# Float16 high and low parts, slots by products and array quarters in a fused attention and mixture-of-experts kernel

## The chip, the cores and the metric

The kernel runs on one core of a Trainium2 chip. The metric is device microseconds for one execution. PE is TensorE, DVE VectorE, ACT ScalarE, POOL GpSimd, SP the engine that issues plain transfers.

## The reference

Local and global attention over q, k, v of shape (4, 8, 768, 64): a query sees the 96 keys that end at itself and the first 8 keys, with a bias that falls with distance. The result, 3072 tokens of 512 numbers, goes through a mixture of eight experts, of which each token takes two:

```python
scores = scale * np.matmul(q, k.transpose(0, 1, 3, 2)) + bias
scores = np.where(keep, scores, -1e9)              # keep = global | local
a = np.exp(scores - max); a = a / (sum + 1e-9)
x = np.matmul(a, v)                                # as (3072, 512)
noisy = x @ w_gate + np.log1p(np.exp(x @ w_noise)) * noise
top2, top2_w = the two largest of 8, softmax of them
for e in range(8):                                 # w1 (8,512,1024), w2 (8,1024,512)
    h = np.maximum(x[mask] @ w1[e], 0.0)
    out[mask] += top2_w * (h @ w2[e])
```

## The kernel before

**Attention.** The work is cut into 24 groups of 128 tokens; a group has four pairs of heads, 96 pairs in all. For a pair, `score` multiplies two blocks of 64 queries with a window of 168 keys (line 480; the first group of each of the 4 batches has 128 keys), in fp32. The two heads of a pair share one product: the query tile `qbuf` holds one head in its upper, the other in its lower 64 rows, with zeros beside them. An fp32 product appears in the trace as two passes on PE. Vector adds the bias and finds the maximum (line 483), Scalar takes the exponential (line 487). `trans` turns the probabilities with four PE transposes per pair (line 499), Scalar copies them out (line 501), `attend` multiplies them with v and a column of ones (line 519, four fp32 products of 65 columns), and Vector divides (lines 525 to 528). The order of each engine is written out by hand in one loop over pairs: transposes of pair n, scores of pair n+2, then `attend` of pair n-2.

**Gate and routing.** After a group's last pair `gate_t`, `gate_l` and `gate_s` turn its tokens, multiply them with the gate weights and leave logits. `gate_l` (line 193) already uses tile positions: four products, each in its own 32 columns of the array. The generator `route`, run a step at a time between other work (`tick`), picks two experts per token for a run of groups (`SEG`), gives each entry a slot, and POOL scatters token number and weight into a table in DRAM (line 297), which is read back.

**Experts.** For each expert e, 812 slots: 512 as part c=0, 300 as part c=1, gathered from DRAM by POOL in seven tiles (`gather`) and turned by PE in fp32 (`turn`, line 164). Precision is kept with float32r pairs: x, w1, h and w2 are split into a high part (Scalar) and the rest (Vector, `split`), and every product is three: high by high, high by low, low by high. `up` (line 693) makes h, `down` and `down_t` (lines 726 and 736) the output, `back` (line 746) turns part c=1 back, and `put` adds rows into the output in DRAM by an indirect transfer (line 711). Per expert: 96 products of 512 and 96 of 300 columns in `up`, as many in `down` and `down_t`. Weights come as 1 MB halves into three `raw` buffers, issued by SP. While expert e is multiplied, its w2, the next w1 and the next tokens are split.

Of the kernel before, what the change touches and what calls it, by code (L numbers as in the profile page):

```python
# [10 lines left out]
F32 = mybir.dt.float32  # L11
# [11 lines left out]
TA = 4  # L23
TB, MB = 3, 100
CA, CB = TA * P, TB * MB
CAP = CA + CB
DUMP = 512


@with_exitstack  # L30
def tile_local_global_attention_then_moe(
# [25 lines left out]
    TS = N + P  # L57
# [4 lines left out]
    SEG = [(0, 6), (6, 12), (12, 17), (17, 21), (21, NT)]  # L62
# [14 lines left out]

    xd = dram.tile([N + DUMP, Dm], F32, name="xd")
    tbl = dram.tile([E * TS, 2], I32, name="tbl")
    slots = tbl.rearrange("(e r) c -> e r c", e=E)  # L80

    zero = consts.tile([P, Dm], F32, name="zero")
    ident = consts.tile([P, P], F32, name="ident")
    noise_s = consts.tile([P, NT, E], F32, name="noise_s")
# [7 lines left out]
    tok = consts.tile([P, NT, 2], I32, name="tok")  # L92
    tb0 = consts.tile([P, TA, 2], I32, name="tb0")
    tba = consts.tile([P, E, TA, 2], I32, name="tba")
    tbb = consts.tile([MB, E, TB, 2], I32, name="tbb")
    more = consts.tile([1, E + 1], I32, name="more")

    w1h = wts.tile([P, KC, F], FR, name="w1h")
    w1l = wts.tile([P, KC, F], FR, name="w1l")
    xh = [wts.tile([P, KC, CA], FR, name="xh0")]  # L100
    xl = [wts.tile([P, KC, CA], FR, name="xl0")]
# [6 lines left out]
    def load_w(n=1):  # L108
        for _ in range(n):
            if len(asked) == len(order):  # L110
                return
            x, e, h = order[len(asked)]
            asked.append(order[len(asked)])
            if x == 1:
                t = wts.tile([P, KC, F // 2], F32, name="raw", tag="raw", bufs=3)
                src = w1[e, :, h * F // 2:(h + 1) * F // 2].rearrange("(k p) f -> p k f", p=P)
            else:
                t = wts.tile([P, FC // 2, Dm], F32, name="raw", tag="raw", bufs=3)
                src = w2[e, h * F // 2:(h + 1) * F // 2].rearrange("(k p) d -> p k d", p=P)
            nc.sync.dma_start(t, src)  # L120
            raw[x, e, h] = t

    def split(e, x, j, eng=nc.vector):

        t = raw[x, e, j // 4]
        if x == 1:
            t = t[:, :, (j % 4) * P:(j % 4 + 1) * P]
            hi, lo = (y[:, :, j * P:(j + 1) * P] for y in (w1h, w1l))
        else:
            t, hi, lo = t[:, j % 4], w2h[:, j], w2l[:, j]  # L130
        nc.scalar.activation(hi, t, AF.Copy)  # L131
        eng.tensor_sub(lo, t, hi.bitcast(F32))  # L132
        if j % 4 == 3 and (e or x == 2):
            load_w()

    xg = {}

    def rows(e, t):

        if t >= TA:  # L140
            return tbb[:, e, t - TA]
        return tba[:, e, t] if e else tb0[:, t]

    def gather(e, t, n=DUMP + N):
        r = rows(e, t)
        xg[e, t] = gp.tile([r.shape[0], Dm], F32, name="xg", bufs=5)
        nc.gpsimd.indirect_dma_start(
            out=xg[e, t], out_offset=None, in_=xd[:n],
            in_offset=bass.IndirectOffsetOnAxis(ap=r[:, 0:1], axis=0),
# [4 lines left out]
    def spare_bank():  # L154
        spare[0] += 1
        return bank("m" if spare[0] % 2 else "lg", 1)

    def turn(e, t, ps=None):
        x = xg.pop((e, t))
        m = x.shape[0]  # L160
        c, c0 = (0, t * P) if t < TA else (1, (t - TA) * MB)
        ps = (spare_bank() if ps is None else ps)[:, :KC * m].rearrange("p (k t) -> p k t", k=KC)
        for k in range(KC):
            nc.tensor.transpose(ps[:, k], x[:, k * P:(k + 1) * P], ident[:m, :m])
        cols = slice(c0, c0 + m)
        nc.scalar.activation(xh[c][:, :, cols], ps, AF.Copy)
        nc.vector.tensor_sub(xl[c][:, :, cols], ps, xh[c][:, :, cols].bitcast(F32))  # L167

    NZ = 8
# [10 lines left out]
    def gate_t(g):  # L180
        x = XR.pop(g).rearrange("p h d -> p (h d)")
        nc.sync.dma_start(xd[DUMP + g * P:DUMP + (g + 1) * P], x)
        ps = bank("m", 1).rearrange("p (k t) -> p k t", k=KC)
# [5 lines left out]
    def gate_l(g):  # L189
        ps = bank("m", 1)[:, :P]  # L190
# [13 lines left out]
    def route(r):  # L204
# [56 lines left out]
        ent = small.tile([P, SW, 2, 2], I32, name=f"ent{r % 2}")[:, :w]  # L261
        we = ent[:, :, :, 1].bitcast(F32)
        nc.vector.reciprocal(we[:, :, 0], wt[:, :, 0])
        nc.vector.tensor_copy(ent[:, :, :, 0], tok[:, a:z])
        yield
        nc.vector.tensor_mul(we[:, :, 1], wt[:, :, 1], we[:, :, 0])
        yield
        ps = lg[:, NT * 2 * E:]
# [13 lines left out]
        nc.vector.tensor_add(po, po, slot0[:, :w])  # L282
# [8 lines left out]
        sli = small.tile([P, SW, 2], I32, name=f"sli{r % 2}")[:, :w]  # L291
        nc.vector.tensor_copy(sli, sl)
        for i in range(w):
            for _ in range(2 if r else 4):
                yield
            for j in range(2):
                ins = nc.gpsimd.indirect_dma_start(
                    out=tbl, out_offset=bass.IndirectOffsetOnAxis(ap=sli[:, i, j:j + 1], axis=0),
                    in_=ent[:, i, j], in_offset=None, bounds_check=E * TS - 1, oob_is_err=False)
                for o in scat:  # L300
                    tc.declare_no_dep(ins.ins, o.ins, reason="each entry has a slot of its own")
                scat.append(ins)
        if r == CLOSE:

            nc.vector.tensor_scalar(carry[:, 0:1], carry[:, 0:1], float(CA), None, op0=OP.max)
            nc.gpsimd.dma_start(tb0, slots[0, :CA].rearrange("(p t) c -> p t c", t=TA))
            for _ in range(12):
                yield
            for t in range(TA):
                gather(0, t, DUMP + z * P)  # L310
                yield

    scat = []


    with ExitStack() as actx:
# [8 lines left out]
        def load_qk(b, j, i0):  # L325

            if i0 == 0:
                qs[b, j] = qbuf[j]
# [23 lines left out]
        if windowed:  # L352
            vpb = [ac.tile([NP + NG, HD], F32, name=f"vp{j}") for j in range(4)]
            qbuf = [ac.tile([P, 2 * NBH, KC, 2, Q], F32, name=f"qbuf{j}") for j in range(2)]
            load_qk(0, 0, 0)
# [32 lines left out]
            def clear(e, j, n):  # L388
                for x in range(2):
                    e.memset(qbuf[j][(1 - x) * D:(2 - x) * D, n, :, x], 0.0)  # L390

# [3 lines left out]
            clear(nc.vector, 0, slice(0, 2))  # L395
# [16 lines left out]
            AW = WIN + Q  # L412
            abuf = [ac.tile([P, 2, AW], F32, name=f"a{j}") for j in range(4)]
            for t in abuf:
                for x in range(2):
                    nc.gpsimd.memset(t[:, x, (1 - x) * WIN:(1 - x) * WIN + Q], 0.0)
            clear(nc.gpsimd, 0, slice(2, 2 * NBH))
# [3 lines left out]
        if windowed:  # L421
            load_v(2)
            clear(nc.gpsimd, 1, slice(0, 2 * NBH))

        def gate_consts():
            nc.vector.memset(wgn, 0.0)
# [5 lines left out]
        def route_consts():  # L432
# [8 lines left out]
            nc.gpsimd.iota(slot0, pattern=[[0, SW], [TS, E]], base=0, channel_multiplier=0,  # L441
                           allow_small_or_imprecise_dtypes=True)
            nc.gpsimd.iota(tok, pattern=[[P, NT], [0, 2]], base=DUMP, channel_multiplier=1)

        def empty_table():
            nc.gpsimd.memset(zero, 0.0)
            j = E * TS // P
            ent0 = ac.tile([P, j, 2], I32, name="ent0")
            nc.gpsimd.memset(ent0, 0)
            nc.gpsimd.iota(ent0[:, :, 0], pattern=[[1, j]], base=0, channel_multiplier=j)  # L450
            nc.vector.tensor_scalar(ent0[:, :, 0], ent0[:, :, 0], DUMP - 1, None, op0=OP.bitwise_and)
            nc.sync.dma_start(tbl.rearrange("(p j) c -> p j c", p=P), ent0)
            o = xd[:DUMP].rearrange("(p r) d -> p r d", p=P)
            nc.sync.dma_start(o, zero[:, None, :].to_broadcast(o.shape))
# [6 lines left out]
        def tick():  # L461
            beat[0] += 1
            active[:] = [(x, r) for x, r in active if r < CLOSE and beat[0] % 2 or next(x, 0) is None]
# [6 lines left out]
        def score(n):  # L470
            g, hp, b, i = geo(n)
            w = WIN if i else P
            j, i0 = divmod(i, NBH)
            ps = bank("sc", 2)[:, :2 * w].rearrange("p (s w) -> p s w", s=2)
            ns = aw.tile([P, 2, WIN], F32, name="ns", bufs=3)
            mx = aw.tile([P, 2], F32, name="mx", bufs=4)
            A[n] = abuf[n % 4]
            for s in range(2):
                k0 = i0 * KB + s * Q if i else NP + NG
                nc.tensor.matmul(ps[:, s], qs[b, j][:, 2 * i0 + s, hp], ks[b, j][:, hp, k0:k0 + w],  # L480
                                 start=True, stop=True)
            for s in range(2):
                nc.vector.tensor_tensor_reduce(  # L483
                    out=ns[:, s, :w], in0=ps[:, s], in1=bias[:, hp, s] if i else bias0[:, hp, s],
                    scale=-scale, scalar=3e38, op0=OP.add, op1=OP.min, accum_out=mx[:, s:s + 1])
                c = s * Q if i else AW - P
                nc.scalar.activation(A[n][:, s, c:c + w], ns[:, s, :w], AF.Exp, bias=mx[:, s:s + 1], scale=-1.0)  # L487
                tick()

        def trans(n):  # L490
            g, hp, b, i = geo(n)
            w = 2 * P if i else P
            ps = bank("at", 2)[:, :2 * w]
# [404 lines left out]
```

## Time and profile before

| | us |
|---|---|
| median of 3 runs (lowest, highest) | 862.3 (860.43, 867.2) |
| profiled execution, first to last instruction | 824.2 |
| attention stage, to the first product of expert 0 | 0 to 207 |
| experts, to the last product | 207 to 813 |
| period of one expert in the middle (439.60 to 514.51) | 74.9 |

The runs' time covers more than the span that the profile shows: the median lies 38.1 us above it. The page gives the busy time of each engine; the timeline gives starts, and the distance from one product's start to the next is its real price, since products overlap and their ends are modelled.

### The profile page before, as it was taken

How to read it: one execution, taken by the hardware profiler on the slowest of the kernel's cores; microseconds unless marked ns; L12 is line 12 of the kernel's file. 1: busy time of each engine (PE TensorE's matmuls, PEld its weight loads, DVE VectorE, ACT ScalarE, POOL GpSimd, SP SyncE). 2: the span in 40 equal slices, each digit the busy share in tenths (PEclk: the TensorE clock that was granted, in tenths of full speed). 3: DMA queues.
4: the chain of work that ended last, by engine and by line, in shares of the span. 5: the costliest groups of instructions: out<-in, count | busy, mean ns of one | idle time of the engine just before them, and what ended most of it. 6: DMA issues, size and time to landing. Idle time of an engine off the chain costs nothing. (4 is left out here: it accounts for less than half of the span.)

```text
span 824.2 us, 14072 instructions
## 1 busy us (share of the span) xinstructions
PE 800.4 (97%) x5265; PEld 722.0 (88%) x5265; DVE 323.9 (39%) x1116; ACT 346.9 (42%) x736; POOL 228.4 (28%) x219
## 2 busy tenths in 40 slices
PE   6999999999998999999999999999999999999994
PEld 6999999999787989898888989898988889898983
DVE  6446656656731434133323423342333334233400
ACT  5778777676422443233333323333333333223311
POOL 4002250353637140314122221403141231302023
PEclk9999999999999999999999999999999999999997
DMA  9899698795366252434343443524443543432014
GB/s 218 215 284 292 163 194 191 176 211 156 116 130 125 66 148 72 108 115 94 113 101 84 120 96 78 139 87 79 121 116 95 100 90 106 96 78 30 2 24 62
DMA packets 86663, 100.73 MB, mean 122 GB/s; under 512 B 35626, under 2 KB 48170, under 8 KB 86586
## 3 DMA queue, kind: packets, MB, share of 16 engines
q1 hardware_dynamic: 71322, 73.05, 33.0%
q0 software_dynamic: 15264, 26.69, 18.0%
q8 instruction: 44, 0.72, 0.4%
q14 instruction: 33, 0.27, 0.1%
HBM read 71.46 MB, written 28.24 MB: 121 GB/s over the span
## 5 line engine op out<-in xcount | busy, mean ns | idle before, releaser
L711 POOL DMA_INDIRECT out_dram<-y,tba x28 | 44.6, 1592 | 257.2 <-ACT y L710 257.2
L726 PE MATMUL av<-w2h,hh 128*128 128x512 f32 x256 | 102.7, 401 | 0.0
L726 PE MATMUL av<-w2h,hl 128*128 128x512 f32 x256 | 101.3, 396 | 0.0
L726 PE MATMUL av<-w2l,hh 128*128 128x512 f32 x256 | 101.1, 395 | 0.0
L132 DVE TENSOR_TENSOR w1l<-raw,w1h 128x512 fp32r<-128x512 f32 x56 | 38.3, 690 | 148.0 <-ACT w1h L131 148.0
L487 ACT ACTIVATE a<-ns,mx 128x168 f32<-128x168 f32 (+1 forms) x192 | 73.0, 423 | 39.8 <-DVE mx L483 38.0
L693 PE MATMUL sc<-xh,w1h 128*128 128x512 f32 (+1 forms) x256 | 89.6, 350 | 0.0
L693 PE MATMUL at<-xh,w1h 128*128 128x512 f32 (+1 forms) x256 | 89.4, 349 | 0.0
L693 PE MATMUL at<-xl,w1h 128*128 128x512 f32 (+1 forms) x256 | 88.6, 346 | 0.3 <-DVE xl L167 0.3
L693 PE MATMUL at<-xh,w1l 128*128 128x512 f32 (+1 forms) x256 | 88.7, 346 | 0.0
L693 PE MATMUL sc<-xh,w1l 128*128 128x512 f32 (+1 forms) x256 | 88.6, 346 | 0.0
L693 PE MATMUL sc<-xl,w1h 128*128 128x512 f32 (+1 forms) x256 | 88.5, 346 | 0.0
L483 DVE CUSTOM_DVE_ANT_0 ns<-sc,bias 128x168 f32<-128x168 f32 (+1 forms) x192 | 55.7, 322 | 71.2 <-ACT at L501 33.8
L711 POOL DMA_INDIRECT out_dram<-y,tbb x24 | 38.2, 1591 | 147.2 <-ACT y L710 146.8
L736 PE MATMUL av<-hh,w2h 128*128 128x300 f32 x256 | 78.9, 308 | 0.0
L736 PE MATMUL av<-hl,w2h 128*128 128x300 f32 x256 | 76.9, 300 | 0.0
L736 PE MATMUL av<-hh,w2l 128*128 128x300 f32 x256 | 76.9, 300 | 0.0
L704 DVE SCALAR_TENSOR_TENSOR hl<-sc,hh 128x300 fp32r<-128x300 f32 (+1 forms) x62 | 35.8, 578 | 102.9 <-ACT hh L703 102.9
L480 PE MATMUL sc<-ks,qbuf 128*128 128x168 f32 (+1 forms) x384 | 70.0, 306 | 5.8 <-DMA qbuf<-in_q 5.8
L703 ACT ACTIVATE hh<-sc 128x300 fp32r<-128x300 f32 (+1 forms) x62 | 31.5, 508 | 100.1 <-PE sc L693 100.1
L710 ACT ACTIVATE y<-av,tba 128x512 f32<-128x512 f32 x28 | 19.3, 689 | 125.4 <-issue 106.2
L519 PE MATMUL av<-vs,at 128*128 128x65 f32 x384 | 70.7, 273 | 0.0
(144 smaller groups left out, 1679.6 us busy)
## 6 DMA issues: line engine op xcount, KB each, us to landing
raw<-in_w SPq DMA_DIRECT2D x32, 1024.0 KB
out_dram<-zero SPq DMA_DIRECT2D x14, 512.0 KB
vs<-in_v SPq DMA_DIRECT2D x24, 260.0 KB
qbuf<-in_q SPq DMA_DIRECT2D x48, 128.0 KB
xd<-xr SPq DMA_DIRECT2D x24, 256.0 KB
ks<-in_k SPq DMA_DIRECT2D x20, 272.0 KB
vp<-in_v SPq DMA_DIRECT2D x20, 195.0 KB
ks<-in_k SPq DMA_DIRECT2D x4, 464.0 KB
```

What stands on the lines that cost most here:

```text
L132: eng.tensor_sub(lo, t, hi.bitcast(F32))
L480: nc.tensor.matmul(ps[:, s], qs[b, j][:, 2 * i0 + s, hp], ks[b, j][:, hp, k0:k0 + w], start=True, stop=True)
L483: nc.vector.tensor_tensor_reduce(out=ns[:, s, :w], in0=ps[:, s], in1=bias[:, hp, s] if i else bias0[:, hp, s], scale=-scale, scalar=3e38, ...
L487: nc.scalar.activation(A[n][:, s, c:c + w], ns[:, s, :w], AF.Exp, bias=mx[:, s:s + 1], scale=-1.0)
L519: nc.tensor.matmul(ps[:, h % 4], x[:kk, s * w + c0:s * w + c0 + P], t[:kk, c], start=kk < P or not i, stop=kk == P)
L693: nc.tensor.matmul(ps, w[:, k, fs], x[c][:, k], start=n == 0, stop=n == 3 * KC - 1)
L703: nc.scalar.activation(hh[c][:, f], ps, AF.Relu)
L704: nc.vector.scalar_tensor_tensor(hl[c][:, f], ps, 0.0, hh[c][:, f].bitcast(F32), op0=OP.max, op1=OP.subtract)
L710: nc.scalar.activation(y, ps, AF.Copy, scale=r[:, 1:2].bitcast(F32))
L711: ins = nc.gpsimd.indirect_dma_start(out=out, out_offset=bass.IndirectOffsetOnAxis(ap=r[:, 0:1], axis=0), in_=y, in_offset=None, bounds_ch ...
L726: nc.tensor.matmul(ps, x[0][:, f, cols], w[:, f], start=n == 0, stop=n == 3 * FC - 1)
L736: nc.tensor.matmul(ps, w[:, f, cols], x[1][:, f], start=n == 0, stop=n == 3 * FC - 1)
```

## The change

All experts' operands become float16 pairs instead of float32r pairs. So that nothing underflows, each weight matrix gets a scale, a power of two from its largest absolute value (`scales`: Vector reductions over 1024 columns, two small PE operations), and each token row another (`ready`); `put` takes both out again. Gathered tiles are scaled and split on Vector and Scalar before they are turned (`ready`, `rest`), and turned by SP with a transposing transfer from SBUF to SBUF (`turn`); PE turns only expert 0's tiles, in float16 (`turn_pe`). Weights have two sets of buffers and five `raw` buffers. Part c=1 has tiles of 128, 128 and 44 rows.

Slots: no scatter. For each of the 48 entries per lane, Vector and POOL make two one-hot tiles, and PE adds their products into a table in PSUM; `find` reads token numbers off it. A token's weights are stored beside it in `xd`, whose rows grow from 512 to 520 numbers.

Attention goes two pairs at a time. Scores are products of 64 rows and 64 columns in the four quarters of the array, without zeros in q; q is loaded with one transfer where there were two. `trans` turns three squares of 128 per pair where it turned four. `attend` has eight products per pair where it had four, each with 64 output rows, in halves of the array and then in quarters. Scores are made for pairs n+4 and n+5. Four of the eight early `zero_out` transfers move into expert 0.

```diff
-    SEG = [(0, 6), (6, 12), (12, 17), (17, 21), (21, NT)]
+    SEG = [(0, 6), (6, 11), (11, 16), (16, 20), (20, NT)]
...
+    def scales(e, x):
...
+        for i in range(4):
...
+            nc.vector.tensor_reduce(m[:, i:i + 1], t[:, i % 2 * n:(i % 2 + 1) * n], op=OP.max, axis=AX.X,
+                                    apply_absolute_value=True)
+            yield
...
+        nc.tensor.transpose(ps[:4, :P], m, ident)
...
+        nc.tensor.matmul(ps[:, :4], one4, d4, start=True, stop=True)
...
     def split(e, x, j, eng=nc.vector):
...
-        nc.scalar.activation(hi, t, AF.Copy)
-        eng.tensor_sub(lo, t, hi.bitcast(F32))
+        nc.scalar.activation(hi, t, AF.Copy, scale=s)
...
+            eng.scalar_tensor_tensor(lo, t, s, hi, op0=OP.mult, op1=OP.subtract)
...
-            nc.tensor.transpose(ps[:, k], x[:, k * P:(k + 1) * P], ident[:m, :m])
...
-        nc.vector.tensor_sub(xl[c][:, :, cols], ps, xh[c][:, :, cols].bitcast(F32))
...
+    def ready(e, t):
...
+        nc.vector.tensor_reduce(c, x[:, :Dm], op=OP.add, axis=AX.X, apply_absolute_value=True)
+        nc.vector.tensor_scalar(c, c, 2.0 ** (1 - X_UP), TINY, op0=OP.mult, op1=OP.max)
+        nc.vector.tensor_scalar(u.bitcast(I32), c.bitcast(I32), EXP, EXP, op0=OP.bitwise_and, op1=OP.bitwise_xor)
...
+        nc.scalar.activation(y[:m, :Dm], x[:, :Dm], AF.Copy, scale=u)
...
+    def rest(e, t):
...
+        nc.vector.scalar_tensor_tensor(y[:m, Dm:], x[:, :Dm], u, y[:m, :Dm], op0=OP.mult, op1=OP.subtract)
...
+    def turn(e, t):
+        nc.sync.dma_start_transpose(out=place(t, P if t < TT - 1 else MP), in_=xp.pop((e, t)))
...
-                ins = nc.gpsimd.indirect_dma_start(
-                    out=tbl, out_offset=bass.IndirectOffsetOnAxis(ap=sli[:, i, j:j + 1], axis=0),
...
+                (nc.vector if j else nc.gpsimd).tensor_scalar(x, row, slf[:, 0, i, j:j + 1], None, op0=OP.is_equal)
+                nc.vector.tensor_scalar(y, col, slf[:, 1, i, j:j + 1], val[:, a + i:a + i + 1],
+                                        op0=OP.is_equal, op1=OP.mult)
...
+        for i, (x, y) in enumerate(marks):
+            nc.tensor.matmul(ps, x, y, start=i == 0, stop=i + 1 == len(marks))
...
-            for x in range(2):
-                nc.sync.dma_start(qs[b, j][x * D:(x + 1) * D, n, :, x].rearrange("p n k t -> p (n k) t"),
-                                  q[b, j, x, :, n].rearrange("p n k t -> p (n k) t"))
+            nc.sync.dma_start(qs[b, j][:, n], q[b, j].rearrange("x d n k t -> (x d) n k t")[:, n])
...
-                nc.tensor.matmul(ps[:, s], qs[b, j][:, 2 * i0 + s, hp], ks[b, j][:, hp, k0:k0 + w],
-                                 start=True, stop=True)
...
+                for m, ps, i, hp, w, qq, kk, i0 in both:
...
+                    r = slice(hp % 2 * D, (hp % 2 + 1) * D)
+                    for y in range(2):
+                        c = hp // 2 * 2 + y
+                        nc.tensor.matmul(ps[y * Q:(y + 1) * Q, s], qq[r, 2 * i0 + s, c], kk[r, c, k0:k0 + w],
+                                         start=True, stop=True, tile_position=(hp % 2 * D, y * Q))
...
+            cols = (0, 2 * WIN - P, NP + NG) if i else (0, P)
...
-                    nc.tensor.transpose(p4[:, :, c, s * Q:(s + 1) * Q], x[:, s, a:a + P], ident)
...
+                nc.tensor.transpose(ps[:, j * P:(j + 1) * P], x[:, a:a + P], ident)
...
+                    parts = (0, 0, vp[g], 0, NP + NG), (0, 1, vs[g], 0, P), (1, 0, vs[g], 0, Q), (1, 1, vp[g], Q, NP + NG)
...
+            run.sort(key=lambda x: x[:3])
...
+                nc.tensor.matmul(ps[y * Q:(y + 1) * Q, h % 4], w, t, start=id(x) in first, stop=id(x) in final,
+                                 tile_position=(r, y * Q))
...
-            for n in range(NPAIR + LAG):
+            for n in range(0, NPAIR + LAG, 2):
```

## Rows read from the trace of the kernel before

**Rows 1.** The page, part 1: busy us of an engine, share, instructions.

```profile
span 824.2 us, 14072 instructions
...
PE 800.4 (97%) x5265; PEld 722.0 (88%) x5265; DVE 323.9 (39%) x1116; ACT 346.9 (42%) x736; POOL 228.4 (28%) x219
```

**Rows 2.** Busy time by stretch: length, PE, PEld, DVE, ACT, POOL, clock, DMA share, GB/s.

```profile
0.00:205.00 205.00, 197.48 (x1846) 189.65 (x1846) 121.97 (x745) 147.00 (x354) 60.50 (x91) 1.00 0.87 210
205.00:290.00 85.00, 80.20 (x471) 69.86 (x471) 36.36 (x92) 28.32 (x57) 39.30 (x34) 1.00 0.48 113
290.00:740.00 450.00, 450.00 (x2548) 398.52 (x2547) 149.16 (x250) 151.92 (x291) 112.83 (x84) 1.00 0.42 101
```

**Rows 3.** Timeline of PE, one pair in attention: start, us, what.

```profile
129.98 0.64 PE L499 MATMUL at<-ident,a 128*128 128x128 f32 x4
130.46 0.74 PE L480 MATMUL sc<-ks,qbuf 128*128 128x168 f32 x4
131.03 0.33 PE L519 MATMUL av<-vp,at 104*128 104x65 f32 x2
...
131.87 0.60 PE L499 MATMUL at<-ident,a 128*128 128x128 f32 x4
```

**Rows 4.** Timeline of PE around the gate product in column tiles.

```profile
78.24 0.39 PE L519 MATMUL av<-vs,at 128*128 128x65 f32 x2
78.55 0.42 PE L193 MATMUL m<-xt,wgn 128*32 128x128 f32 x8
78.91 0.55 PE L499 MATMUL at<-ident,a 128*128 128x128 f32 x3
```

**Rows 5.** Timeline of PE in `down`, with one turned tile behind it.

```profile
558.18 0.39 PE L726 MATMUL av<-w2h,hl 128*128 128x512 f32 x1
...
562.38 0.40 PE L726 MATMUL av<-w2h,hl 128*128 128x512 f32 x1
562.61 0.60 PE L164 MATMUL lg<-ident,xg 128*128 128x128 f32 x4
562.96 0.48 PE L726 MATMUL av<-w2h,hh 128*128 128x512 f32 x1
563.28 0.39 PE L726 MATMUL av<-w2l,hh 128*128 128x512 f32 x1
```

**Rows 6.** Timeline of PE in `up`, part c=0.

```profile
515.21 0.39 PE L693 MATMUL at<-xh,w1h 128*128 128x512 f32 x1
...
517.02 0.40 PE L693 MATMUL at<-xh,w1l 128*128 128x512 f32 x1
```

**Rows 7.** Timeline of PE in `up`, part c=1.

```profile
539.80 0.30 PE L693 MATMUL sc<-xh,w1h 128*128 128x300 f32 x1
...
541.59 0.30 PE L693 MATMUL at<-xl,w1h 128*128 128x300 f32 x1
```

**Rows 8.** Groups by line and shape, Vector: busy us, mean ns, idle before.

```profile
L704 DVE SCALAR_TENSOR_TENSOR hl<-sc,hh 128x512 fp32r<-128x512 f32 x30 | 20.8, 692 | 64.9 <-ACT hh L703 64.9
L704 DVE SCALAR_TENSOR_TENSOR hl<-sc,hh 128x300 fp32r<-128x300 f32 x32 | 15.1, 471 | 37.9 <-ACT hh L703 37.9
L228 DVE SCALAR_TENSOR_TENSOR p<-p,t 128x40 f32<-128x40 f32 x6 | 1.2, 197 | 0.1
```

**Rows 9.** Transfers by issue: count, median us from issue to landing.

```profile
xg<-xd,tba POOLq DMA_INDIRECT x28, 3.8
out_dram<-y,tba POOLq DMA_INDIRECT x28, 7.6
```

**Rows 10.** The page's transfer rate in 40 slices, and its packets.

```profile
GB/s 218 215 284 292 163 194 191 176 211 156 116 130 125 66 148 72 108 115 94 113 101 84 120 96 78 139 87 79 121 116 95 100 90 106 96 78 30 2 24 62
DMA packets 86663, 100.73 MB, mean 122 GB/s; under 512 B 35626, under 2 KB 48170, under 8 KB 86586
```

More of the change, by code (lines that the diff above doesn't have):

```diff
@@ L768, in tile_local_global_attention_then_moe @@
+            up(0, 0, f, f < 3, {4: gate_t, 8: gate_l, 11: gate_s} if f == 0 and windowed else {})
+            for j in range([0, 0, 0, 2, 3, 4, 6, 7][f], [0, 0, 2, 3, 4, 6, 7, 8][f]):
+                split(0, 2, j)
+        for _ in pending[1]:
+            pass
         for t in range(TB):
             gather(0, TA + t)
-        for t in range(TA - 1):
+        for t in range(2):
+            gather(1, t)
+        weigh(0, 0, TA)
+        for t in range(TA):
             down(0, t)
-        for t in range(TB):
-            turn(0, TA + t, bank("sc", 2) if t == TB - 1 else None)
@@ new lines, in tile_local_global_attention_then_moe @@
+            if t == 1:
+                step(1)
+                for j in range(TB):
+                    ready(0, TA + j)
+                    if j:
+                        rest(0, TA + j - 1)
+                rest(0, TA + 2)
+                for j in range(2, 5):
+                    gather(1, j)
+            if t == 2:
+                step(1)
+                ready(1, 0)
+                step(1, 2)
+            if t == 3:
+                rest(1, 0)
+                turn(1, 0)
+                ready(1, 1)
@@ new lines, in tile_local_global_attention_then_moe @@
+        for t in range(TB):
+            turn_pe(0, TA + t, bank16("sc", 3) if t == TB - 1 else None)
+        for j in range(5, 7):
+            gather(1, j)
+        for f in range(FC):
+            up(0, 1, f)
+            if f in (0, 2, 4):
+                rest(1, 1 + f // 2)
+                turn(1, 1 + f // 2)
+            if f in (0, 2):
+                ready(1, 2 + f // 2)
+            if f == 0:
+                load_w(2)
+            if f not in (0, 2):
+                step(1)
+        ready(1, TA)
@@ new lines, in tile_local_global_attention_then_moe @@
+        for j in range(KC):
+            down_t(0, j)
+            step(1)
+            if j < TB:
+                rest(1, TA + j)
+                turn(1, TA + j)
+                if j + 1 < TB:
+                    ready(1, TA + j + 1)
+        weigh(0, TA, TT)
+        for e in range(1, E):
+            last = e + 1 == E
+            for f in range(FC):
+                up(e, 0, f)
+                if f < TB:
+                    back(e - 1, f)
+                step(e, [0, 0, 0, 1, 0, 1, 2, 2][f])
+                if f == 2 and not last:
+                    for t in range(5):
+                        gather(e + 1, t)
+            weigh(e, 0, TT)
+            for f in range(FC):
+                up(e, 1, f)
+                if f < 2:
+                    step(e, 2)
+                elif f < 6:
+                    step(e + 1)
+                if not last:
+                    if f in (4, 6):
+                        ready(e + 1, f // 2 - 2)
+                    if f in (5, 7):
+                        rest(e + 1, f // 2 - 2)
+                        turn(e + 1, f // 2 - 2)
+                        gather(e + 1, f // 2 + 3)
```

589 lines of the change are left out of this document (343 added, 246 removed).

## The prediction

> **What bounds the kernel now.** I read the page first: PE is busy 97% of the span, Vector 39%, Scalar 42% [rows 1]. Shares over a whole span hide stages, so I looked at stretches next [rows 2]. In attention (0 to 205 us) PE is busy 197 us, but Scalar has 147 and Vector 122 too; in the experts (290 to 740) PE is busy without a break and Vector a third of the time. Third, the timeline of PE, where only starts count. A pair of heads takes 1.89 us from the start of its transposes to the next pair's: 0.48 for four transposes, 0.57 for the scores (four passes of 0.143), 0.84 for eight passes of `attend`, 0.105 each [rows 3]. `attend` streams only 65 columns, and its passes still cost nearly what a transpose of 128 does: loading 128 fp32 columns into the array sets its pace, while the scores go by their stream. In the experts eighteen products of 512 columns in `down` take 4.20 us, 0.233 each [rows 5], eight in `up` 1.81, 0.226 each [rows 6], thirteen of 300 columns 1.79, 0.138 each [rows 7]. The clock is at its full level, 2.4 GHz, in all three stretches [rows 2]. So the kernel is a queue of PE work, and what the change is worth is what it takes out of that queue, until another engine is late.
>
> **Experts.** *Products.* Count and columns stay (512 and 300; three products per float pair), the type changes. At 2.4 GHz 512 columns stream in 0.213 us and 300 in 0.125; the float32r products lie 0.013 to 0.020 above that. No row has a wide float16 product. The bounds: nothing saved (0 us), or all but a small gap. The fp32 scores, which stream too, lie only 0.0025 above their stream (0.1425 against 2 x 168 columns = 0.140) [rows 3], and I take that, as the nearest row that streams without a penalty for the type: 0.216 and 0.1275. Then 768 products in `down` save 0.0173 each (13.3 us), 768 in `up` 0.010 (7.7), 1536 narrow ones 0.010 (15.7): 36.7 us.
>
> *Turning.* A turned tile costs PE from where the next product would have started, 562.61, to 562.96, and the product behind it comes 0.32 later where 0.233 is usual: 0.44 us [rows 5]. 49 tiles (seven experts, seven tiles) leave PE: 21.6 us. They go to SP's queue as transposing transfers. No row shows one. Its landing is bounded by nothing and by some multiple of the two transfers of about the same bytes, 3.8 us for a gathered tile and 7.6 for an added one [rows 9]; I take 4. It is hidden: tile 3 is issued two `down` steps into expert e, six steps before the first product of e+1, some 22 us. On SP each waits for `rest` on Vector, and behind it wait the weight loads, which have five buffers instead of three. Expert 0's seven tiles stay on PE, eight narrow transposes instead of four wide ones: no difference.
>
> *Scales.* Sixteen matrices, each one transpose and one tiny fp32 product, three passes of some 0.11 us as in [rows 3]: 5.3 us added to PE. Their inputs come from Vector one step earlier in program order, with a `down` or an `up` between, so PE doesn't wait.
>
> *Cover.* Vector gains eight reductions over 1024 columns per expert. A row of 512 takes 0.692 us and one of 300 0.471, so a column is 1.04 ns and a reduction 1.22 us: 9.8 us. `ready` adds 7 x (0.69 + two small ones, 0.2 each), 7.6. Vector had 149 us in six experts [rows 2], 25 each; with 2 for the rest 44 of some 68 us. Hidden, if bursts don't hold up the evacuation of PSUM. Sum for the experts: -36.7 - 21.6 + 5.3 = **-53 us**.
>
> **Attention.** I count a double step of two pairs, 3.78 us now. *Transposes*: six instead of eight, 0.72. *Scores*: sixteen quarter passes; if four run side by side, four rounds of 0.143, 0.57. *`attend`*: 32 passes with half the columns to load; two side by side make 16 rounds. A round costs between half of 0.105 (half the columns) and all of it; I take 0.06, near the lower end, since the load sets today's price: 0.96. That parts of the array work side by side is in the trace: `gate_l`'s eight passes in four column tiles take 0.36 us, entry and exit included, where eight passes of `attend` take 0.84 [rows 3, 4]. *Changes of mode* are the price: before those passes PE starts 0.20 after the last product where 0.11 is usual, of the 0.36 some 0.15 is no stream, and the three transposes behind take 0.06 more than theirs [rows 4]: 0.30 for in and out, 0.15 each. A double step has three (halves, quarters, whole): 0.45. The Trainium skill (TensorEngine Tiling, Key Properties) says that a change of tiling mode, not of tile, drains the engine; it speaks against this change, the rows agree, and the price is the rows' own. Sum 2.70, 1.08 less, in 40 double steps 43 us. The eight double steps with one block of keys go from 2.2 (0.48 + 0.86 + 0.84) to 1.84 (0.48 + 0.48 + 0.43 + 0.45), 3 us in all. PE alone would give 46.
>
> Vector doesn't allow that. It has 122 us there and gets 35 more: 9.8 for the reductions of two matrices, 72 marks at some 0.22 (40 columns are 0.197 [rows 8]) 15.8, `ready` and `rest` of four tiles 6, weights 3. 157 of the 159 that would be left can't all be hidden. I assume that it can fill nine tenths of a stage, as its work comes in bursts behind each score; the stage is then 174 instead of 205: **-31 us**. Scalar loses 80 x 0.1 by narrower copies and stays below Vector. The transfers: 210 GB/s over 205 us [rows 2] would be 247 over 174, and slices of 284 and 292 occur [rows 10]; q's pieces of 256 B, most of the 35,626 packets under 512 B, become 2 KB. Moving four `zero_out` transfers costs nothing, with expert 0's queue at half load. POOL loses the scatters and gains two passes per early `split`: not on the path. The routing's way to the first gathers is shorter without a table in DRAM, worth at most the few us of PE idle between 205 and 290 (85.0 - 80.2); I count none. Start and tail stay.
>
> **The sum.** 824.2 - 53 - 31 = 740. The median lies 38.1 above the span, so **778 us**, own range 755 to 800 for Vector's share between eight and ten tenths and rounds of 0.053 to 0.08.
>
> **Rivals.**
> (1) *PE stays the pace in attention.* For it: nine tenths is my estimate alone; PE itself reaches 197 of 205 [rows 2]. Attention gives all of its 46: 824.2 - 53 - 46 + 38.1 = 763.
> (2) *Two parts in one PSUM bank wait for each other.* `attend`'s second half puts rows 0 to 63 and 64 to 127 of the array into one bank; `gate_l`'s tiles share rows, so no row shows this. Eight more rounds of 0.06 per double step, 40 times: +19, 797. The Trainium skill has this as a rule (TensorEngine Tiling, Gotcha 1: different row tiles can't access the same bank at once).
> (3) *Float16 products keep the float32r distance.* For it: nothing here shows otherwise. Then only the turning counts, -16 in the experts: 815.
> (4) *The transposing transfers become the bound.* Seven per expert, one behind the other, decide from 68/7 = 9.7 us each on; the added row's 7.6 [rows 9] is under it, 11 is not far. At 11, 77 us per expert, +9 seven times: 839. The Trainium skill is of two minds: VectorE: DVE Perf Modes, The three transpose paths, gives 1309 ns for one square of 128, of which a tile has eight (10.5 us, an estimate), and Advanced Engine Details and Errata, X-Bar Transpose, says that such a transfer is as fast as a plain one; no run here shows either yet.
> (5) *Slower: the parts don't run side by side.* Place: `score` and `attend` on PE. If the tile positions only cut the work into pieces, a double step is 0.72 + 16 x 0.143 + 32 x 0.06 + 0.45 = 5.38, 1.60 more than now: +64, with the short steps +68, and the experts' -53: 877. It decides from a double step of 4.9 us on, where attention loses what the experts gain. Against it: [rows 4].
>
> **How the numbers follow.** Forecast 0.50, (1) 0.12, (2) 0.10, (3) 0.10, (4) 0.07, (5) 0.08, others 0.03. The range, 742 to 838, leaves out (5), half of (4) and a tail below (1): under 2 in 10. About 1% (8.6 us) is what a measurement can tell from no change. All but (5) lie below 853: faster 0.90, same 0.03, slower 0.07.
>
> **What the profile will show.** Line by line: float16 products 0.216 and 0.1275 apart in the experts, an expert's period near 68 us; in attention a double step near 3.5 us with the gate's share in it (4.1 now: 205 less some 7 us of start, over 48), groups of four scores starting within some 0.03 us, a step of about 0.15 at each change of tile; Vector busy about nine tenths of attention, and PE with short waits for Vector's or Scalar's results; `turn`'s transfers landing within 4 us, and no product waiting for one. The prediction is wrong if score passes follow one another at 0.143, if the first `up` of an expert waits for SP's transfers, or if Vector's bursts hold PSUM banks so long that PE idles inside the experts.

## The result, and the profile after

The changed kernel takes **757.2 us** (median of four runs, 755.5 to 757.9), the kernel before 861.4 beside it (860.0 to 867.2): a ratio of 0.876, 95% interval 0.872 to 0.881. Forecast were 778, range 742 to 838.

The kernel before has two paces, 825 to 834 us in some sessions and 860 to 869 in others, the same chip among both, its span some 1.7 us below its time each time; the span of 824.2 us on which the prediction rests belongs to the quicker pace, and the changed kernel and its variants with small edits have medians of 750 to 757 us in sessions of either. The profiled run after took 757.93 us with a span of 756.2.

Busy time after, the page's first part and its packets:

```profile
span 756.2 us, 16302 instructions
PE 719.7 (95%) x6199; PEld 452.0 (60%) x6199; DVE 485.3 (64%) x1655; ACT 347.0 (46%) x744; POOL 208.7 (28%) x201
...
DMA packets 107671, 112.56 MB, mean 149 GB/s; under 512 B 53216, under 2 KB 66224, under 8 KB 107584
```

And by stretch, in the columns of [rows 2], from two questions to the same trace:

```profile
0.00:205.00 205.00, 179.14 (x2987) 138.72 (x2988) 156.31 (x926) 133.91 (x365) 49.52 (x78) 0.94 0.74 235
205.00:290.00 85.00, 81.78 (x492) 46.19 (x491) 57.54 (x153) 35.90 (x65) 44.46 (x37) 0.98 0.57 133
290.00:740.00 450.00, 450.00 (x2682) 263.01 (x2680) 271.42 (x577) 175.24 (x312) 108.42 (x82) 1.00 0.58 115
...
9.00:72.00 63.00, 62.94 (x1170) 50.68 (x1172) 44.23 (x271) 49.87 (x145) 1.26 (x7) 1.00 0.85 261
72.00:193.00 121.00, 100.50 (x1722) 79.59 (x1718) 96.83 (x574) 78.15 (x208) 39.43 (x41) 0.91 0.65 209
```

PE (TensorE) was busy 197 of the first 205 us and is now busy 179; the loss is not spread evenly. From 9 to 72 us it has no gap; from 72 to 193 it stands still for a sixth of the time and its mean granted clock falls to 0.91, though Vector, at 97 of 121 us, is not full over that stretch as a whole. In the experts PE stays without a break and Vector is at 60%.

**Where the 68 us between the two spans come from.** The first product of expert 0 is issued at 193.1 us (207.4 before), the last at 748.4 (812.4). Attention gave 14.3 us, the experts 605.0 - 555.3 = 49.7, and 4.0 lie behind the last product (11.8 before, 7.8 after).

The products, PE's timeline after (start, duration, what), to be set beside [rows 5 to 7]; from the first to the last line of a pair there are eighteen steps in `down`, three in `up` and eighteen of the narrow ones:

```profile
304.49 0.38 PE L890 MATMUL av<-w2h,hh 128*128 128x512 f16 x1
...
308.38 0.38 PE L890 MATMUL av<-w2h,hh 128*128 128x512 f16 x1
...
281.91 0.38 PE L857 MATMUL at<-xx,w1l 128*128 128x512 f16 x1
...
282.56 0.38 PE L857 MATMUL at<-xx,w1l 128*128 128x512 f16 x1
...
262.03 0.29 PE L900 MATMUL av<-hh,w2h 128*128 128x300 f16 x1
...
264.33 0.29 PE L900 MATMUL av<-hh,w2h 128*128 128x300 f16 x1
```

3.89 / 18 = 0.216 in `down`, 0.65 / 3 = 0.217 in `up`, 2.30 / 18 = 0.128 for the narrow ones: float16 lies 0.003 to 0.004 above the streams of 0.213 and 0.125 that the forecast counted, where float32r lay 0.013 to 0.020 above them [rows 5 to 7].

Attention where PE sets the pace, PE's timeline after:

```profile
53.59 0.22 PE L664 MATMUL av<-vs,at 64*64 64x65 f32 x1
53.60 0.22 PE L664 MATMUL av<-vp,at 40*64 40x65 f32 x1
53.65 0.22 PE L664 MATMUL av<-vs,at 64*64 64x65 f32 x1
53.66 0.22 PE L664 MATMUL av<-vp,at 40*64 40x65 f32 x1
...
61.14 0.63 PE L285 MATMUL sc<-ident,xr 128*128 128x128 f32 x4
61.61 0.82 PE L637 MATMUL at<-ident,a 128*128 128x128 f32 x6
...
67.37 0.31 PE L285 MATMUL sc<-ident,xr 128*128 128x128 f32 x1
```

Two passes of `attend` start 0.01 us apart, from different rows of the array into different rows of one PSUM bank, and the next two 0.06 later: they run side by side. From L285 to L285, two double steps with the gate's products, is 6.23 us; the trace of before has 8.58 for the same four pairs. The tenth such group begins at 73.6 us, 54.5 after the first (74.1 in the trace before): 19.6 us won in nine intervals. From there to the 24th it is 121.2 us against 115.7: nothing more is won, and 5.5 are given back.

The largest wait: the chain of waits after (start, length, what), then SP's queue (SPq, where a time is how long the instruction holds the queue) and GpSimd in the same stretch, then Vector's and PE's timelines with the idle time before the instruction in brackets:

```profile
106.46 6.12 DMA xd<-xr
112.64 0.04 issue
112.68 0.15 DVE xr L672
```

```profile
93.36 0.35 SPq L461 DMA_DIRECT2D qs<-in_q  x1
105.02 0.68 SPq L584 DMA_DIRECT2D xd<-zero  x1
...
106.46 1.33 SPq L282 DMA_DIRECT2D xd<-xr  x1
...
103.36 1.17 POOL L206 TENSOR_TENSOR w1l<-raw,w1h 128x512 f16<-128x512 f32 x1
104.46 0.53 POOL L582 MEMSET zero<- 128x512 f32 x1
```

```profile
112.68 0.42 DVE L672 TENSOR_TENSOR xr<-av,den 128x256 f32<-128x256 f32 x1 [2.86 <-DMA xd<-xr]
...
114.80 0.58 PE L299 MATMUL lg<-sel,ls 128*128 128x16 f32 x2 [5.79 <-DVE ix L344]
```

Read it backwards. Vector's `xr` at 112.68 needs one of two buffers, which the store `xd<-xr` empties; that store was issued only at 106.46, because SP's queue stood at `xd<-zero` from 93.7 to 105.0 (in the view of waits 10.8 us of it are for POOL's `zero`), and POOL's zeroing stood behind its halves of the splits, 2.7 us each. Vector's queue is in order too, so scores and routing stop with `xr`, and PE stands from 109 to 115. Of PE's 5.8 us Vector itself waits 2.9; from 101.0 to 109.8, ahead of its wait, it is busy 8.63 of 8.80 us, so the rest is Vector's own queue of scores, routing and maxima. The same L285 group that takes 0.63 above takes 1.09 at 115.22 behind this wait, with a granted clock of 0.50, the lower of its two levels, from 115 to 120 us.

### The profile page after: what moved, and what is told of

Same layout as the page of the kernel before. It is cut to its first block, busy times and chain, and to the rows that moved or that the text cites. A ratio compares the mean times of both kernels' runs of the same rounds, so it can differ in the third digit from the quotient of the medians.

```text
span 756.2 us, 16302 instructions
## 1 busy us (share of the span) xinstructions
PE 719.7 (95%) x6199; PEld 452.0 (60%) x6199; DVE 485.3 (64%) x1655; ACT 347.0 (46%) x744; POOL 208.7 (28%) x201
## 2 busy tenths in 40 slices
DMA packets 107671, 112.56 MB, mean 149 GB/s; under 512 B 53216, under 2 KB 66224, under 8 KB 107584
## 4 chain that ended last, share of the span: by engine, by line
PE 69%; issue 12%; DVE 10%; DMA 3%; POOL 2%; ACT 2%; SPq 0%; POOLq 0%; DVEq 0%; ACTq 0%
PE av L890 16%; PE at L857 15%; PE sc L857 14%; PE av L900 10%; PE av L664 5%; PE at L637 3%; PE sc L616 3%; POOL out_dram L875 2%; DVE ns L623 2%; PE sc L285 1%; DVE entry L409 1%; DMA qs<-in_q 1%; DMA xd<-xr 1%; DMA raw<-in_w 1%; PE sc L293 1%
## 5 line engine op out<-in xcount | busy, mean ns | idle before, releaser
L875 POOL DMA_INDIRECT out_dram<-y,ids x56 | 88.6, 1583 | 211.7 <-ACT y L874 207.2
L857 PEld LDWEIGHTS <-w1h 128*128 128x128 f16 x1024 | 100.1, 99 | 70.5 <-issue 2.2
L857 PE MATMUL at<-xx,w1h 128*128 128x300 f16 (+1 forms) x512 | 128.5, 339 | 2.0 <-ACT xx L266 1.9
L857 PE MATMUL sc<-xx,w1h 128*128 128x300 f16 (+1 forms) x512 | 126.5, 336 | 0.0
L890 PE MATMUL av<-w2h,hh 128*128 128x512 f16 x256 | 97.1, 379 | 0.0
L890 PE MATMUL av<-w2l,hh 128*128 128x512 f16 x256 | 97.0, 379 | 0.0
L890 PE MATMUL av<-w2h,hl 128*128 128x512 f16 x256 | 97.0, 379 | 0.0
L857 PE MATMUL at<-xx,w1l 128*128 128x512 f16 (+1 forms) x256 | 86.7, 339 | 0.0
L857 PE MATMUL sc<-xx,w1l 128*128 128x512 f16 (+1 forms) x256 | 85.8, 335 | 0.0
L149 DVE TENSOR_REDUCE wmx<-raw 128x1 f32<-128x1024 f32 x64 | 76.4, 1205 | 0.0
L900 PE MATMUL av<-hl,w2h 128*128 128x300 f16 x256 | 74.1, 290 | 0.0
```

Source lines behind the costliest of these rows:

```text
L149: nc.vector.tensor_reduce(m[:, i:i + 1], t[:, i % 2 * n:(i % 2 + 1) * n], op=OP.max, axis=AX.X, apply_absolute_value=True)
L857: nc.tensor.matmul(ps, w[e % 2][:, k, fs], xx[c][:, x + k, :hh[c].shape[2]], start=n == 0, stop=n == 3 * KC - 1)
L875: ins = nc.gpsimd.indirect_dma_start(out=out, out_offset=bass.IndirectOffsetOnAxis(ap=rows(e, t), axis=0), in_=y, in_offset=None, bounds_c ...
L890: nc.tensor.matmul(ps, x[0][:, f, cols], w[e % 2][:, f], start=n == 0, stop=n == 3 * FC - 1)
L900: nc.tensor.matmul(ps, w[e % 2][:, f, cols], x[1][:, f], start=n == 0, stop=n == 3 * FC - 1)
```

## The experiments

Time, and ratio to the kernel before in the same session, with its interval; before took 827 us beside the first four and the last, 862 to 864 beside the others.

**1. The kernel before, again.** No edit.

> The kernel before, run again, to see what lies outside its span: 862 us were shown beside a span of 824.2 us, 38 us, while the changed kernel's profiled execution takes 757.93 us with a span of 756.2, 1.7 us. Theory A: the profiled execution of before was a quicker one than those that were timed, and the usual span is near 860, with some 2 us outside; then the span to compare 756 with is 860, and the change took about 104 us out of the span. Theory B: the program before has some 38 us outside its span (its span stays at 824), and the change took 68 us out of the span and 36 us from outside.

826.9 us (824.95 to 833.96), ratio 0.9987 [0.9964, 1.001], spans 823 to 832. Neither theory held as put: no more than some 1.7 us lies outside the span, and 824.2 is no odd run but the usual span at the quicker pace. The 38 us are a second pace of the kernel before.

**2. The zeroing back at beat 12.** A beat is a pair's turn in attention's loop. The zeros fill spare rows of `xd`; the kernel before has this zeroing at beat 12, so the move to 58 is a part of the change, which the forecast doesn't name.

```
-            at(58, empty_rows)
+            at(12, empty_rows)
```

> The changed kernel with the zeroing of the dump rows issued at beat 12 instead of beat 58. Theory A (SP's queue in order): the store of the zeros waits 10.8 us for GpSimd's zeroing, which is queued behind GpSimd's halves of the splits and the marks, and everything behind it on SP's queue comes late; the 6.1 us of idle PE at 106 to 115 us and the stretch at half the clock behind it go: 746 to 751 us. Rival B (the forecast's step: Vector's busy share alone sets attention): the idle time only shows up elsewhere, 755 to 759 us.

750.1 us (749.4 to 750.4), 0.9046 [0.9011, 0.908]. SP's wait for POOL's zeros falls from 10.8 to 2.9 us, and the interval at 109 us between the starts of PE's products from 6.1 to 3.3. What is left of it, 3.0 us of waiting, is again for Vector's `ix`, and Vector is full there (run 2's busy time by stretch, columns of [rows 2]):

```profile
103.00:112.80 9.80, 6.15 (x127) 4.59 (x125) 9.66 (x54) 7.34 (x20) 7.39 (x6) 1.00 0.81 263
```

This is the fastest version run; that it beats the changed kernel itself rests on run 8, which had it in the same session.

**3. All tiles turned by PE, where the transposing transfer was issued.** `turn = turn_pe`.

> The changed kernel with the tiles of experts 1 to 7 turned by TensorE as those of expert 0 are, so that SP issues no transposing transfer. Theory A (the forecast's term): 49 tiles cost TensorE 0.44 us each, +21.6 us, 779 us (776 to 784). Rival B: the transposing transfers held something up that now runs free, and little or nothing is lost: 755 to 765 us. Rival C: Vector's and Scalar's copies out of PSUM come in bursts that hold TensorE up: over 790 us.

994.9 us (992.2 to 996.3), 1.201 [1.196, 1.206]. Rival C, but not by the copies out of PSUM: the chain shows PE itself waiting for the tile.

```profile
445.72 1.42 DVE w1l L208 x2
447.13 0.66 DVE xp L249
447.80 0.07 DVE wv L250
447.87 0.59 PE lg L261 x4
448.46 7.54 PE av L888 x24
```

PE's queue is in order, the tile comes from Vector behind two splits, and the `down` behind the turn could start only then; it took 7.54 us instead of 24 x 0.216 = 5.2, the granted clock being 0.50 from 448.4 to 452 us. A transposing transfer waits on SP's queue, and in the changed kernel's trace no product waits for what stands there behind it. The edit measured a queue, not a price; hence run 7.

**4. Score products of one quarter behind each other.** The loops of `score` in the order m, y, s instead of s, m, y.

> The changed kernel with the score products of a double step issued so that the two of one quarter of the array follow each other, instead of a product for each quarter in turn; the products are the same. Theory A (four quarters run side by side only if neighbours in the queue use different quarters, and TensorE is the pace in attention): the eight products take five intervals of 0.285 us instead of two, +0.86 us in 40 double steps, +34 us: 785 to 795 us. Rival B (side by side, but Vector is the pace in attention): TensorE's extra time is taken from its idle time, +0 to +12 us: 757 to 769 us. Rival C (order makes no difference to how parts run side by side): 755 to 759 us, with the scores of a double step still in 0.57 us.

751.9 us (751.1 to 754.2), 0.9074 [0.9035, 0.9113]. Rival C on the main point, the order of the passes; the time lies 3 us under its range, in a session without the changed kernel itself. The sixteen passes start at 54.03, then in fours about 0.142 apart, as many at once as in the changed kernel; the interval of two double steps is 6.38 us instead of 6.23. By these starts a quarter's passes wait for their own quarter and not for their neighbours in the queue.

**5. The changed kernel itself.** No edit.

> The changed kernel itself, on the chip of the runs sent with it. The kernel before took 861 us beside the first runs of the changed kernel and 827.6 us beside the first experiments, with 1.7 us outside the span both times. Theory A: two chips run before at two paces; the changed kernel, 757 us beside the 861, comes to 0.876 of whatever before takes here (725 us beside 827). Theory B: the difference hits before alone (something in it that the change took out), and the changed kernel takes 752 to 758 us on any chip, 0.91 of before where before takes 827.

756.5 us (754.4 to 758.6), 0.8758 [0.8723, 0.8794]: Theory B as far as it goes. The kernel itself was not run beside before's quicker pace; runs 2 and 4, near relatives, were, and gave 750 and 752.

**6. Expert 0's maxima over 32 columns.**

```
-            nc.vector.tensor_reduce(m[:, i:i + 1], t[:, i % 2 * n:(i % 2 + 1) * n], ...
+            o = n if e else 32
+            nc.vector.tensor_reduce(m[:, i:i + 1], t[:, i % 2 * n:i % 2 * n + o], ...
```

> The changed kernel with expert 0's eight maxima taken over 32 columns each instead of 1024, so that 8 x 1.1 us of Vector's work leave attention; most of that maximum is left out of the computation. Theory A (the forecast's step: Vector's work sets the pace where TensorE waits): 6 to 10 us less than the changed kernel itself beside it. Rival B (SP's queue and its transfers set the waits, Vector is only busy): within 3 us of it.

755.7 us (754.7 to 757.0), 0.8743 [0.8713, 0.8773], against 0.8758 for the kernel itself: Rival B. Vector was relieved of 7 us (99.64 to 92.72 busy between 72 and 193 us) and nothing came of it; PE's interval at 107 us is there with its 6.1 us, as Vector now waits 4.4 us for `xr`'s store instead of 2.9.

**7. All tiles turned by PE, one step later.** `turn` keeps its tile and turns that of the call before; the last one is turned ahead of the last `down`.

> The changed kernel with the tiles of experts 1 to 7 turned by TensorE, and each put one step later in TensorE's queue than in the run where the turning stood right behind the step that makes the tile (that run took 995 us, and its chain shows TensorE waiting for Vector and Scalar before each tile). Theory A (the price of turning itself, 49 tiles of 0.44 us): 21.6 us more than the changed kernel itself, 18 to 27. Rival B (the queue in order is the price: even a step later TensorE waits for Vector's bursts): 40 us more or beyond. Rival C (the transposing transfers cost something that goes now): under 15 us more.

808.9 us (806.9 to 810.2), 0.9348 [0.9314, 0.9382], 52 us above the kernel itself: Rival B in sum, and Theory A's price inside it. PE's timeline has one tile of each sort:

```profile
461.98 0.29 PE L861 MATMUL sc<-xx,w1l 128*128 128x300 f16 x1
462.76 0.40 PE L268 MATMUL sc<-ident,xp 128*128 128x128 f16 x4 [0.48 <-ACT xp L242]
465.36 0.40 PE L268 MATMUL sc<-ident,xp 128*128 128x128 f16 x4 [2.20 <-DVE wv L250]
465.59 0.38 PE L894 MATMUL av<-w2h,hh 128*128 128x512 f16 x1
...
470.88 0.61 PE L268 MATMUL lg<-ident,xp 128*128 128x128 f16 x8
471.32 0.38 PE L894 MATMUL av<-w2h,hh 128*128 128x512 f16 x1
```

The tile at 470.88, eight float16 passes, costs 0.447 us; so do most others, 0.30 the narrow one. An expert's period is 75.6 us instead of 68.3: 6 x 0.447 + 0.30 = 2.98 of the 7.3 are turning, the rest are two waits per expert, 3.0 us at the tile above (0.65 ahead of it, 2.38 in its middle) and 1.2 at its fifth.

**8. Short maxima and early zeroing.** Runs 2 and 6 together.

> The changed kernel with both expert 0's maxima over 32 columns (most of that maximum left out) and the zeroing of the dump rows at beat 12. Theory A (two separate causes of waiting): its gain over the changed kernel is the sum of both, 6 to 10 us from the maxima and 5 to 7 from the zeroing: 11 to 17 us. Rival B (one cause hides the other, the later of two waits counts): no more than the larger one alone, 6 to 9 us.

750.6 us (749.0 to 751.2), 0.8678 [0.8648, 0.8708]: Rival B. Beside run 6 in the same session the zeroing is worth 5.1 us, with the intervals apart; the maxima again nothing in time, next to run 2, though PE's interval there falls from 3.3 to 2.0 us.

**9. The kernel before, for a trace at its slower pace.** No edit.

> The kernel before once more, for a trace of it on a chip where it takes 862 us, if this chip is one. Its mean granted clock was 0.97 there and 0.993 where it takes 827 us. Theory A: on the slow chips TensorE falls to the lower level of 1.2 GHz in many short stretches between products in the experts, at full busy share, and the 35 us are spread over them. Theory B: they lie in attention and the stretch behind it (0 to 290 us), and the experts keep 74.9 us each. On a chip with 827 us this run says nothing new.

861.5 us, span 859.8, clock 0.974, on the chip that had shown 827. Theory B. Busy time by stretch, columns of [rows 2], run 1 and then this one:

```profile
104.00:122.00 18.00, 18.00 (x171) 17.20 (x171) 11.05 (x66) 13.51 (x36) 11.99 (x12) 1.00 0.93 191
...
166.00:186.00 20.00, 20.00 (x199) 19.42 (x197) 11.11 (x78) 14.42 (x34) 10.99 (x12) 1.00 0.91 191
```

```profile
104.00:122.00 18.00, 11.43 (x93) 10.22 (x91) 4.09 (x26) 5.79 (x16) 11.97 (x12) 0.80 0.69 166
122.00:166.00 44.00, 41.60 (x381) 40.58 (x382) 24.55 (x159) 30.69 (x72) 0.00 (x0) 0.93 0.53 132
166.00:186.00 20.00, 9.11 (x84) 8.08 (x83) 6.38 (x37) 5.89 (x17) 11.74 (x12) 0.75 0.62 150
```

In both runs POOL (the fifth busy time) issues twelve scatters into the slot table in each of the two short stretches: a train of twelve each time here, in run 1 parts of two trains in the second stretch. Here PE loses 7 and 11 us in them and works at a lower clock in and behind them (0.80, 0.93 and 0.75); beside a third train, from 202 us on, it loses 5 more. What holds PE up the profile doesn't say: it names nothing but "issue" for PE's longest wait there, 9.6 us. Expert 0's first product comes at 242.6 us instead of 207.4, the last 605.1 us after it, as in the quicker trace (605.0): all 35 us lie in attention.

**10. PE's small steps later.** With the zeroing at beat 12:

```
-            for x, places in (1, (34, 36, 42, 44, 46, 48)), (2, (58, 60, 66, 68, 70, 72)):
+            for x, places in (1, (32, 34, 36, 38, 46, 50)), (2, (58, 60, 66, 68, 76, 82)):
...
+        for _ in range(3 if r < CLOSE else 0):
+            yield
         for i in range(w):
             nc.tensor.matmul(pos[:, i], upper, ohs[:, i], start=True, stop=i == 0)
```

> The changed kernel with the zeroing at beat 12 and, in attention, TensorE's small steps further behind the Vector work that they need: the transposes and products of expert 0's scales four beats later (their reductions two to eight beats earlier for the first matrix), the products for positions of the first two routes three steps later. Theory A (TensorE's queue in order waits at these places, 0.7 + 0.9 + 1.2 + 1.7 + 1.2 us in the trace with the zeroing at beat 12): 744 to 747 us, 4 to 6 below the 750 of the zeroing alone. Rival B (Vector's backlog is what TensorE waits for, and a later place only moves the wait): 749 to 752 us.

757.4 us (756.7 to 759.5), 0.877 [0.8726, 0.8814]: Rival B, and worse. The waits come back elsewhere, two of them larger (PE's timeline, the wait in brackets):

```profile
138.23 0.37 PE L153 MATMUL sc<-ident,wmx 128*4 128x128 f32 x1 [1.71 <-DVE mx L625]
154.01 0.58 PE L299 MATMUL lg<-sel,ls 128*128 128x16 f32 x2 [3.58 <-DVE tab L422]
```

**11. Early zeroing and quarters in turn.** Runs 2 and 4 together.

> The changed kernel with the zeroing at beat 12 and the score products of one quarter behind each other. Theory A (the order among the quarters makes no difference: in the trace of that order alone four passes start within 0.03 us all the same, in rounds of 0.142): as with the zeroing alone, 749 to 752 us. Rival B (the products in quarters are free to drift apart and end a little sooner, 751.9 us alone against 756.5 of the changed kernel on another chip): 745 to 748 us.

754.3 us (753.1 to 758.1), 0.8741 [0.8692, 0.8789]. Not the gain of Rival B, and above Theory A's range; 4 us over run 2, of another session, where the order's 0.15 us in each of 24 intervals would be 3.6. That is near, and no more than that across sessions.

**12. The kernel before without its scatters.** The 48 scatters of `route` are left out and the table is filled at the start:

```
-                ins = nc.gpsimd.indirect_dma_start(
-                    out=tbl, out_offset=bass.IndirectOffsetOnAxis(ap=sli[:, i, j:j + 1], axis=0),
...
+            nc.gpsimd.iota(ent0[:, :, :, 0], pattern=[[0, E], [1, j]], base=DUMP, channel_multiplier=j)
+            nc.sync.dma_start(tbl.rearrange("(e p j) c -> p e j c", e=E, p=P), ent0)
```

> The kernel before without GpSimd's 48 scatters of slot entries into the table in DRAM: the table is filled beforehand so that expert e's slot s holds token s. It leaves out the routing of tokens to slots; gathers, products and added rows keep their number and size. In the trace of before at 862 us, transfers stop and TensorE idles 5.3, 3.7 and 9.9 us while two trains of twelve scatters run (104 to 122 and 166 to 186 us), and the clock is at the lower level behind each; in the trace at 827 us the same trains hold nothing up. Theory A (these trains are what before loses where it takes 862 us, and the change, which has no scatters, took that out): 818 to 828 us whichever pace before shows beside it. Rival B (the trains are only where another cause shows, which holds transfers up anyway): over 850 us where before takes 862. Where before takes 827 beside it the run can't tell the two apart.

820.1 us (819.8 to 820.4), 0.9914 [0.9883, 0.9945], with before at 826.6 beside it. The time is Theory A's and its five runs lie within 0.6 us, where before's eight spread over 6; but the kernel before was at its quicker pace beside it, and the run can't tell A from B.

## Why the prediction was right, and where it was not

The range held; the mechanism held in the experts; two terms missed by 17 and 36 us with opposite signs, so part of the closeness of 757 to 778 is luck.

**Products, -36.7**: measured as forecast, 0.216 and 0.128. Rival (3) is refuted. **Turning, -21.6**: the price of a tile on PE is 0.447 us (run 7), forecast 0.44. The transposing transfer holds SP's queue for 1.2 us (the tile's own view after: shortest, median and longest in ns), where the plain issues shown above hold it for 0.35 to 1.33; its landing, forecast as 4 us, can be read in run 4 alone, which has the same transfers, for six of the 49: 3.1 to 10.1 us, median 5.4. First the changed kernel's view, then run 4's two, the second with KB each and the median from issue to landing:

```profile
L257 SPq DMA_TRANSPOSE xx<-xp x36: 1232/1232/5189, 307.8 to 672.3; - x36
```

```profile
DMA to landing us min/median/max: 3.1/5.4/10.1
...
xd<-xr SPq DMA_DIRECT2D x24, 256.0 KB, 7.9
xg<-xd,ids POOLq DMA_INDIRECT x56, 3.7
out_dram<-y,ids POOLq DMA_INDIRECT x56, 4.9
xx<-xp SPq DMA_TRANSPOSE x42, 5.2
```

The forecast's "within 4 us" did not hold, but no product waits for such a transfer, and the expert's period is 68.3 us: rival (4) is refuted. Of the two statements of the Trainium skill weighed there, these landings, among those of the plain transfers beside them, fit Advanced Engine Details and Errata, X-Bar Transpose; the estimate of 10.5 us, eight times the 1309 ns of VectorE: DVE Perf Modes, lies above all six. What the forecast did not see is that the transfer also keeps the tile's lateness out of PE's queue; runs 3 and 7 put 30 us and more on that. **Scales, +5.3**: mis-sized. The transpose at 281.37 is followed by the next product 0.11 later, and the tiny product with its change in and out takes another 0.41 in run 2's trace (four intervals of 0.309, 0.133, 0.180 and 0.225 in place of two of 0.216); 0.52 each, 7.3 us for the fourteen in the experts: 2.0 of the 3.3 us by which the experts fell short of -53. **Cover**: Vector's 253 us between 290 and 680 make 44 of 68 us per expert, as forecast, and PE has no gap there.

**Attention, -31**: the step that failed is "it can fill nine tenths of a stage". PE's own pace came out a little better than forecast (6.23 us for two double steps with the gate; 8.58 before, so 2.35 won where 2 x 1.08 was counted), which refutes rivals (2) and (5): the rule of the Trainium skill (TensorEngine Tiling, Gotcha 1) does not show in these rows, where passes from two row tiles into different rows of one bank start together. But rival (1) did not follow, and Vector's share of the stage was not the reason: it was 80% from 72 to 193 us, and 7 us less work for it gave nothing (run 6). What stood in the place of that step are queues in order that meet: 22 intervals over 0.45 us between the starts of PE's products up to 208 us, 28.0 us in all (5, with 3.5 us, in the trace before). Vector is one of these queues, full for some 10 us at a time (run 2), and what the share hid is who waits behind it there. The largest of these meetings was SP behind POOL, "Moving four `zero_out` transfers costs nothing" and "not on the path" having been said of SP's and POOL's queues without a word on the other zeroing, which the change moved to beat 58, or on who waits behind it; run 8 beside run 6 prices it at 5 us. The rest are in the main PE's small steps behind Vector's routing; run 10 moved some and lost. How much of the rest a better order could win is open: a third `xr` buffer, the obvious next try, wasn't tried.

**The 38.1 us above the span**: wrong. It was added as something that lies around the span; it lay inside attention, in runs of the slower pace, and the change has no scatters into a table that could bring it about. Worked from the quicker pace throughout, the forecast would have been 740 + 1.7 = 742, and the 756.2 found in place of 740 are 16.7 us in attention and 3.3 in the experts, less 4.0 behind the last product, which the forecast left as it was. Part of the ratio of 0.876 is thus before's slower pace: against the 826.9 us of run 1 the 757.2 would be 0.92, an estimate across sessions. That the stretches of the scatter trains are where before loses most of its 35 us is shown (run 9); that they cause it is argued, since run 12 met the quicker pace.

**Packets.** The forecast had q's short pieces go; they did, packets under 512 B falling from 28,912 (0 to 207 us before) to 3,408 (0 to 193 after). That the page's count rose from 35,626 to 53,216 all the same is the experts': 42,236 fall between 290 and 680 us, where the transposing transfers run. That these are theirs the views don't say.

## What to carry to other kernels

Before adding a constant between a span and a median, find out whether it lies outside the span: run the kernel before again and compare spans. A share of busy time over a stage says little about an engine whose queue is in order, and hides the places where it is full; ask of each instruction that waits on another engine what is queued behind it, and behind that (here a zeroing on POOL held SP, SP a store, the store a buffer, the buffer Vector, and Vector PE). And work that leaves a full engine for a transfer takes its lateness along: that was worth more here than the work.

## What the runs showed that was not expected

Beside the same twelve scatters in a row on POOL, PE was busy 11.4 of 18 us in one session and 18.0 in another, with the same program on the same chip; whether the scatters cause it isn't shown. Passes in quarters of the array ran four at once in either order in the queue (rounds of 0.142 us, 0.07 us a double step between the orders). A transposing transfer held SP's queue for 1.2 us and landed after 3.1 to 10.1: the first time is not the second. And a wait costs twice: behind the 6 us at 109 us the same four transposes take 1.09 us instead of 0.63, and the mean granted clock from 72 to 193 us is 0.91, where it was 1.00 from 9 to 72.
